# A gated spectral mixer on one core: first half products from 32-bit operands, row tiles normalised one by one, new due times, and a last down product in three parts

## The chip, the cores and the metric

The kernel runs on one core of a Trainium2 chip. The core has five engines with a queue each: PE (matrix products, with its weight loads shown as PEld), DVE (vector work), ACT (activations and copies), POOL, and SP, which here issues all transfers between DRAM and the core's memory. Each engine works through its queue in order; semaphores make one wait for another. The metric is the device time of one execution in microseconds (us), the median of several runs.

## What is computed

The reference has two halves that meet in the last line. `x` is 1 x 2048 x 512.

```python
def _A_ref(x, w_r, w_i):                       # 2-D real FFT over (S, D), filter, inverse
    X = rfft2(x); X = X * (w_r + 1j * w_i); return irfft2(X)

def _B_ref(x, W_gate, W_up, W_down):           # 512 -> 1376 -> 512
    gate = einsum("bsd,df->bsf", x, W_gate)
    up   = einsum("bsd,df->bsf", x, W_up)
    gate = gate * (gate > 0)
    return einsum("bsf,fd->bsd", gate * up, W_down)

xn = _layernorm(x)
return x + _A_ref(xn, A_w_r, A_w_i) * _silu(_B_ref(xn, B_W_gate, B_W_up, B_W_down))
```

## The kernel before

**Tiles.** The 2048 rows are 16 row tiles of 128, loaded two at a time as x0 to x7. The feed-forward half works on four blocks c of four row tiles each (512 columns of PE's output), and on eleven feature tiles f of 128 (the last has 96). `product(c, f, i)` is one such product, i = 0 for the gate weights and 1 for the up weights; its result is the PSUM tile gu{c}_{f}_{i}. `rectify` and `hidden` make the hidden tile h from it, `down(c, f, rows)` multiplies h with the down weights into dn{c}_{row tile}, and `gate` applies the silu.

**Precision.** Everything is multiplied as pairs of 16-bit numbers, a high part and a remainder ("low"): a product of two such pairs takes three passes (`PASSES`: high x high, high x low, low x high). For the first layer one product is 4 blocks of 128 input features x 3 passes = 12 instructions. So before a product can start, x must be normalised, transposed and split (xT, high by ACT and low by DVE), and the weights must be scaled and split: `squares` on ACT sums the squares of the raw weights, `group_scale` adds them over the partitions with a product with `ones` on PE and makes a power of two of it on DVE (p), `group_split` writes the high part (ACT or DVE) and the low part (DVE) into wgu. Weights come in seven groups, raw0 to raw6, of which 0, 1 and 2 hold one feature tile each.

**The start.** x0 (row tiles 0 and 1) is normalised: `stats` makes mean and variance on DVE, `deviation` the inverse deviation with small DVE steps around a root on ACT, for both row tiles in one go, then `normalise` (row tile 0 on DVE, row tile 1 on ACT). `turn_row` transposes them on PE into head0, from which xT is copied. Block 0's feature tiles 0 and 1 (`HALF` = 2) are multiplied in two halves: row tiles 0 and 1 first, 256 columns, then row tiles 2 and 3 when x1 is there. Until PE has work, `keep_busy` fills it with products of `ones` into the PSUM tile small, 79 of them.

**The transform.** The FFT half is a chain of stages per chunk: first_stage (PE tile s1_, results t1_, written to a DRAM tile A_d), then per chunk q loads `at` from A_d and stages y, xx, z, v (results t9_, written to C_d), then last_stage (ct loads, PE tile s2_). The s, v and y stages use 64-wide parts of PE's array.

**What sets the order.** Each piece of work is a `step` with an engine, a cost, the names it reads and writes, and a due time. `Plan.run` plays all steps through a small model of the engines, buffers and transfers: a free engine takes, of the steps that can begin, the one due first. Products get due times from a running clock (`tick`, from `T0`); transform stages from constants (`FIRST`, `MID`, `LAST` with a constant step each); loads from `LOADS` and a lead. The order so found is then what each engine's queue holds. All instructions pass one helper, so the profile gives line 65 for all of them, and groups are told apart by the names of tiles.

**The end.** The last row tile's down product is made in two parts of 256 columns (`columns`, dn3_3 and dn3_3b), so that silu, product with the transform's result sv, sum with x and the store of the first part run while PE makes the second.

The lines that set the widths and the order of that last row tile:

```python
    return (slice(0, 256), slice(256, D)) if (c, i) == (NBL - 1, 3) else (slice(0, D),)
    order = [(f, 2, 0) for f in range(NFT)] + [(f, 3, part) for part in range(2) for f in range(NFT)]
```

Of the kernel before, what the change touches and what calls it, by code (L numbers as in the profile page):

```python
# [32 lines left out]
T0, DOWN, FIRST, FIRST_STEP, MID, MID_STEP, LAST, LAST_STEP = 1.2, 94.9, 53.3, 17.6, 150.3, 18.1, 292.6, 10.8  # L33
LOADS, LOADX = [4.2, 0, 4.4, None, None, None, None], [-2.7, -0.3]
FOLDS, FOLD_LEAD, MARGIN = ['DVE', 'DVE', 'DVE', 'DVE', 'DVE', 'DVE', 'DVE', 'DVE'], 67.8, 1.95
# [3 lines left out]
BUSY, LATE, PAIR1, PAIR2 = 79, 0.4, 0, 0  # L39
SQUARES, HALF = 32.82, 2  # L40
HURRY, SLOW, SLOW_TO = -2, 1, 20
LOWS = [("DVE", "DVE")] * 8

# [4 lines left out]
def columns(c, i):  # L48

    return (slice(0, 256), slice(256, D)) if (c, i) == (NBL - 1, 3) else (slice(0, D),)  # L50
# [184 lines left out]
def kernel(ctx: ExitStack, tc: tile.TileContext, x, wg, wu, wd, wl, ew, sp, c_r, c_d, c_m, c_x, c_s, out):  # L235
# [39 lines left out]
    warm = cpool.tile([P, 1], F32, name="warm")  # L275
    ACT.activation(warm, ones[:, 0:1], AF.Sqrt)
# [25 lines left out]
    def load_x(c):  # L302
        tile_of(f"x{c}", "k4", [P, 2, D], F32)
        if c == 1:
            after_first(("x1", 0), lambda: T["x1"][:, 0, 0:1])
        for i in range(1 + (c == 0)):
            rows = slice(i, i + 1) if c == 0 else slice(0, 2)
            step("SP", .5, lambda rows=rows: SP.dma_start(T[f"x{c}"][:, rows], x[:, 2 * c + rows.start:2 * c + rows.stop, :]),
                 writes=[(f"x{c}", i)], lead=14 if c else None, kb=256 * (rows.stop - rows.start), lag=2.2, due=(LOADX[c] + i * .01) if c < 2 else None)
# [4 lines left out]
    def stats(c, q, j):  # L314
# [6 lines left out]
        tile_of(f"mv{c}", "mv", [P, 2, 2], F32)  # L321
        for i in range(2):
            step("DVE", .82, lambda i=i: run(i), reads=x_names(c, i), writes=[(f"st{c}", i), (f"mv{c}", i)])

    def deviation(c):

        tile_of(f"q{c}", "q", [P, 4, 2], F32)

        def first():
            q = T[f"q{c}"]  # L330
            DVE.tensor_scalar(q[:, 0], T[f"mv{c}"][:, :, 1], EPS, -4.0 / XS ** 2, op0=ALU.add, op1=ALU.mult)

        def last():
            ve, sq, y, t = (T[f"q{c}"][:, i, :] for i in range(4))
            DVE.reciprocal(y, sq)
            for i in range(2):
                DVE.scalar_tensor_tensor(t[:, i:i + 1], y[:, i:i + 1], ve[:, i:i + 1], y[:, i:i + 1],
                                         op0=ALU.mult, op1=ALU.mult)
            DVE.scalar_tensor_tensor(y, t, 3.0, y, op0=ALU.add, op1=ALU.mult)
            if "ACT" in NORM[c]:  # L340
                DVE.scalar_tensor_tensor(ve, T[f"mv{c}"][:, :, 0], -1.0, y, op0=ALU.mult, op1=ALU.mult)
        step("DVE", .13, first, reads=[(f"mv{c}", 0), (f"mv{c}", 1)], writes=[f"q{c}"], port=True)
        step("ACT", .11, lambda: ACT.activation(T[f"q{c}"][:, 1], T[f"q{c}"][:, 0], AF.Sqrt, scale=-1.0),
             reads=[f"q{c}"], writes=[(f"q{c}", 1)])
        step("DVE", .78 + .14 * ("ACT" in NORM[c]), last, reads=[(f"q{c}", 1)], writes=[(f"q{c}", 2)], port=True)
        return f"q{c}", 0
# [19 lines left out]
    def normalise(c, q, at, engines=("DVE", "DVE")):  # L366
# [9 lines left out]
        for i in range(2):  # L376
            e = engines[i]
            step(e, .62 if e == "ACT" else dve2(512), lambda i=i: run(i), reads=[*x_names(c, i), (f"mv{c}", i), (q, 2)],
# [27 lines left out]
    def turn_row(c, i):  # L406
# [13 lines left out]
        step("PE", .45, run, reads=[(f"xf{c}", i)], writes=[(f"head{c}", i)])  # L420
# [66 lines left out]
    def load_group(g):  # L487
        w = sum(fwidth(f) for f in GROUPS[g])
        for i, src in enumerate((wg, wu)):
            tile_of(f"raw{g}_{i}", "k4", [P, 4, w], F32)  # L490
            if g == 1 and not i:
# [3 lines left out]
                 reads=["go"] if g else [], writes=[f"raw{g}_{i}"], lead=12 if g else None, kb=2 * w, lag=2.5, due=LOADS[g])  # L495
# [11 lines left out]
    def group_scale(g):  # L507
        nf = len(GROUPS[g])
        if g > 1:
# [680 lines left out]
```

## Time and profile before

| What | us |
|---|---|
| Runs: median of 3 (lowest, highest) | 409.06 (409.02, 409.29) |
| Profiled execution: span from first to last instruction | 407.1 |
| Median of the runs less that span | 1.96 |
| PE busy in the span | 401.4 (99%) |
| DVE busy | 304.0 (75%) |
| ACT busy | 188.0 (46%) |
| POOL busy | 46.7 (11%) |

The profile is one execution. Its span runs from the first to the last instruction; what lies around it is part of the runs' time and not in the trace. PE's clock was granted in full throughout (1.000). A row of the timeline is "start, length, engine, line, operation, output <- inputs, partitions x elements, how many", and in brackets the idle time of that engine before it and who ended it. A group's length runs from the start of its first instruction to the end of its last, and products overlap at their ends, so the distance between the starts of two groups is the better price. "PEld" is the weight load of a product, "SPq" the time in which SP issues a transfer.

### The profile page before, as it was taken

Reading aid. Unit: us, or ns where it says so; the run is one execution under the profiler, and the core shown is the slowest. Engines: PE = TensorE matmul, PEld = TensorE weight load, DVE = VectorE, ACT = ScalarE, POOL = GpSimd, SP = SyncE. Lnnn points to the kernel's source line nnn. Section 1 sums busy time; section 2 is a strip of 40 time slices with the busy share of each in tenths; the row PEclk is TensorE's granted clock in tenths of the full one; section 3 lists DMA queues with packets and bytes.
Section 4 is the critical chain, followed back from the end, with each engine's and each line's share of the span. In section 5 each row is a group of like instructions: output and inputs, shape, how many; then the busy total and the mean of one; then the engine's idle time right before and its main releaser. Section 6 shows DMA issues by size and latency. Waiting matters only on the chain.

```text
span 407.1 us, 7606 instructions
## 1 busy us (share of the span) xinstructions
PE 401.4 (99%) x2992; PEld 211.5 (52%) x2992; DVE 304.0 (75%) x647; ACT 188.0 (46%) x358; POOL 46.7 (11%) x72
## 2 busy tenths in 40 slices
PE   8999999999999999999999999999999999999995
PEld 7864444444444445455465455546555444444555
DVE  4897986998798979706987578686792328987974
ACT  4999823743467636222355433534523336242411
POOL 0000000000000000001612032030330008040300
PEclk9999999999999999999999999999999999999999
DMA  7980002218549608690006540324201297563242
GB/s 244 403 304 1 0 2 109 54 52 208 171 152 305 172 15 209 128 291 13 2 0 191 173 144 0 100 92 149 52 2 52 61 242 182 161 185 105 103 156 103
DMA packets 36291, 51.78 MB, mean 127 GB/s; under 512 B 15840, under 2 KB 17600, under 8 KB 36256
## 3 DMA queue, kind: packets, MB, share of 16 engines
q1 hardware_dynamic: 36256, 51.31, 42.5%
q8 instruction: 23, 0.38, 0.4%
q14 instruction: 12, 0.10, 0.1%
HBM read 35.55 MB, written 12.60 MB: 118 GB/s over the span
## 4 chain that ended last, share of the span: by engine, by line
PE 97%; ACT 1%; DVE 1%; issue 0%
PE gu L65 55%; PE dn L65 27%; PE s L65 3%; PE z L65 3%; PE xx L65 3%; PE small L65 2%; PE y L65 2%; PE v L65 2%; PE dn_3b L65 1%; ACT xT L65 1%; ACT wgu L65 0%; PE head L65 0%; DVE xT L65 0%; PE sum L65 0%; DVE p L65 0%
## 5 line engine op out<-in xcount | busy, mean ns | idle before, releaser
L65 PE MATMUL gu<-xT,wgu 128*128 128x512 f16 (+1 forms) x1008 | 213.3, 369 | 0.4 <-DVE xT L65 0.4
L65 PEld LDWEIGHTS <-wgu 128*128 128x128 f16 x1008 | 97.5, 98 | 107.5 <-issue 3.5
L65 PE MATMUL dn<-wds,h 128*128 128x512 f16 (+2 forms) x528 | 115.8, 373 | 0.0
L65 PEld LDWEIGHTS <-h 128*128 128x128 f16 (+1 forms) x561 | 53.7, 98 | 57.3 <-issue 2.0
L65 DVE TENSOR_TENSOR h<-gu,r 128x512 f32<-128x512 f32 (+2 forms) x52 | 33.6, 646 | 24.2 <-PE gu L65 22.9
L65 ACT ACTIVATE h<-h 128x512 f16<-128x512 f32 (+1 forms) x44 | 27.5, 626 | 51.0 <-DVE h L65 51.0
L65 POOL TENSOR_TENSOR po<-tt,tt 128x256 f32<-128x256 f32 x16 | 14.4, 900 | 262.6 <-DVE tt L65 208.7
L65 ACT ACTIVATE r<-gu 128x512 f32<-128x512 f32 (+1 forms) x44 | 26.2, 595 | 36.5 <-PE gu L65 36.3
L65 DVE TENSOR_TENSOR h<-h,h 128x512 f16<-128x512 f32 (+1 forms) x44 | 29.7, 689 | 5.3 <-ACT h L65 5.1
L65 DVE SCALAR_TENSOR_TENSOR tt<-xsp,cw,wt 128x512 f32<-128x512 f32 x32 | 25.3, 847 | 0.0
L65 POOL TENSOR_TENSOR ae<-zz 128x128 f32<-128x128 f32 (+1 forms) x32 | 17.8, 593 | 62.8 <-ACT zz L65 47.9
L65 ACT ACTIVATE g<-dn,cdi 128x512 f32<-128x512 f32 (+1 forms) x16 | 10.6, 673 | 23.9 <-PE dn L65 23.9
L65 PE MATMUL gu<-xT,wgt 128*64 128x256 f16 (+1 forms) x144 | 17.0, 309 | 0.0
L65 DVE TENSOR_TENSOR sv<-sv,g 128x512 f32<-128x512 f32 (+1 forms) x17 | 11.2, 690 | 6.4 <-ACT g L65 6.1
L65 DVE TENSOR_TENSOR t<-v,t 128x1024 f16<-128x1024 f32 x8 | 9.8, 1219 | 7.9 <-ACT t L65 7.9
L65 DVE TENSOR_TENSOR z<-z,z 128x1024 f16<-128x1024 f32 x8 | 9.7, 1218 | 7.5 <-ACT z L65 7.5
L65 ACT ACTIVATE z<-z 128x1024 f16<-128x1024 f32 x8 | 8.2, 1024 | 15.2 <-PE z L65 15.2
L65 POOL TENSOR_TENSOR pf<-tt,tt 128x256 f32<-128x256 f32 x16 | 14.0, 888 | 7.7 <-PE gu L65 7.7
L65 ACT ACTIVATE p<-pf 128x1024 f16<-128x1024 f32 x8 | 8.4, 1056 | 13.0 <-DVE pf L65 13.0
L65 DVE SCALAR_TENSOR_TENSOR wgu<-raw,p,wgu 128x512 f16<-128x512 f32 x20 | 14.4, 745 | 0.1
L65 ACT ACTIVATE xs<-xs 128x1024 f16<-128x1024 f32 x8 | 8.3, 1052 | 12.8 <-DVE xs L65 9.3
L65 ACT ACTIVATE wgu<-raw 128x512 f16<-128x512 f32 x20 | 12.3, 619 | 3.7 <-DMA raw<-in_wg 3.7
(134 smaller groups left out, 430.6 us busy)
## 6 DMA issues: line engine op xcount, KB each, us to landing
A_d<-t SPq DMA_DIRECT2D x16, 256.0 KB, 3.3
rw<-in_wl SPq DMA_DIRECT2D x8, 512.0 KB, 5.1
wt<-in_wl SPq DMA_DIRECT2D x8, 512.0 KB, 4.8
at<-A_d SPq DMA_DIRECT2D x8, 512.0 KB, 4.9
C_d<-t SPq DMA_DIRECT2D x16, 256.0 KB, 3.3
ct<-C_d SPq DMA_DIRECT2D x16, 256.0 KB, 5.6
xt<-in_x SPq DMA_DIRECT2D x16, 256.0 KB, 4.3
out<-xt SPq DMA_DIRECT2D x15, 256.0 KB, 2.1
```

What stands on the lines that cost most here:

```text
L65: return lambda *args, **kw: self.tc.keep_in_program_order(f(*args, **kw))
```

## The change

Four things change.

1. **32-bit half products.** For block 0 and feature tiles 0 and 1, the half for row tiles 0 and 1 is no longer made from split 16-bit numbers. `turn_row` copies the transposed x as 32-bit numbers (xTf0 by ACT, xTf1 by DVE), and `product` multiplies the raw 32-bit weights with it: four 128-column products for each row tile, each weight matrix and each of the two feature tiles, 32 in all. Their scale differs from that of the other half, so `rectify` and `hidden` work on these tiles in two halves with different factors (p and the new `ups`). xT is then split from xTf. Feature tile 1's results move from the tag dn to F.
2. **Row tiles one by one.** For x0, `deviation` runs once for each row tile (`ALONE`), and the statistics of row tile 1 are made by ACT (`STATS`: a sum, its negative mean, a sum of squared differences), not by DVE.
3. **Due times.** The transform stages get a due time each in place of a constant step, loads a lead each, and most constants of the model change. `keep_busy` makes 42 filler products in place of 79.
4. **The end.** The last row tile's down product has three parts of 256, 128 and 128 columns (dn3_3, dn3_3b, dn3_3bb).

```diff
-T0, DOWN, FIRST, FIRST_STEP, MID, MID_STEP, LAST, LAST_STEP = 1.2, 94.9, 53.3, 17.6, 150.3, 18.1, 292.6, 10.8
+FIRSTS = [58.53, 65.2, 93.07, 106.1, 121.7, 135.1, 152.7, 170.3]
...
-BUSY, LATE, PAIR1, PAIR2 = 79, 0.4, 0, 0
+BUSY, LATE = 42, 0.4
...
+ALONE, EVAC, WHOLE = (((0,), (1,)), ((0, 1),)), ("ACT", "DVE"), .95
+HALVES, HEADS, STATS = ('gu', 'F'), [None, 8.91], ((0, 1),)
...
-    return (slice(0, 256), slice(256, D)) if (c, i) == (NBL - 1, 3) else (slice(0, D),)
+    return (slice(0, 256), slice(256, 384), slice(384, D)) if (c, i) == (NBL - 1, 3) else (slice(0, D),)
...
         for i in range(2):
+            if (c, i) in STATS:
+                st, mv, of, junk = (lambda: T[f"st{c}"]), (lambda: T[f"mv{c}"]), (lambda: T[f"x{c}"][:, i, :]), (lambda: T[f"xf{c}"][:, i, 0:D])
+
+                step("ACT", .75, lambda: ACT.activation(junk(), of(), AF.Copy, accum_out=st()[:, 6:7]),
+                     reads=x_names(c, i), writes=[(f"st{c}", 2), (f"xf{c}", i)])
+                step("ACT", .2, lambda: ACT.activation(st()[:, 7:8], st()[:, 6:7], AF.Copy, scale=-1.0 / D),
+                     reads=[(f"st{c}", 2)], writes=[(f"st{c}", 3)])
+                step("ACT", .8, lambda: ACT.activation(junk(), of(), AF.Square, bias=st()[:, 7:8], accum_out=st()[:, 8:9]),
+                     reads=[*x_names(c, i), (f"st{c}", 3)], writes=[(f"st{c}", i), (f"xf{c}", i)])
+                step("DVE", .13, lambda: DVE.tensor_scalar(mv()[:, i, :], st()[:, 6:9:2], 1.0 / D, None, op0=ALU.mult),
+                     reads=[(f"st{c}", i), (f"st{c}", 2)], writes=[(f"mv{c}", i)])
+                continue
...
+        if c == 0:
+            n = f"xTf{i}"
+            tile_of(n, "k2", [P, 4, P], F32)
+            e, act_ = EVAC[i], lambda: ACT.activation(T[n].rearrange("p k r -> p (k r)"), head(), AF.Copy)
+            step(e, (dve if e == "DVE" else act)(512), act_ if e == "ACT" else lambda: DVE.tensor_copy(T[n].rearrange("p k r -> p (k r)"), head()),
+                 reads=[(f"head{c}", i)], writes=[n])
+            of = lambda: T[n].rearrange("p k r -> p (k r)")
+            step("ACT", act(512), lambda: ACT.activation(xt(0), of(), AF.Copy), reads=[n], writes=[(f"xT{c // 2}", j, 0)])
+            step("DVE", dve(512), lambda: DVE.tensor_sub(xt(1), of(), xt(0)), reads=[n, (f"xT{c // 2}", j, 0)],
+                 writes=[(f"xT{c // 2}", j, 1)], port=True)
+            return
...
+        if c == 0 and f < HALF and rows.start == 0:
+            def whole(j):
+                for k in range(4):
+                    matmul(to()[:, j], T[f"raw{g}_{i}"][:, k, :], T[f"xTf{j}"][:, k, :], start=k == 0, stop=k == 3)
+            for j in range(2):
+                step("PE", WHOLE, lambda j=j: whole(j), reads=[f"xTf{j}", f"raw{g}_{i}"], writes=[(name, 0, i)], due=tick(WHOLE))
+            sums[c, f, i] = to, [(name, k, i) for k in range(2)]
+            return
...
+        elif c == 0 and f < HALF:
+            step("DVE", stt(256), lambda: DVE.scalar_tensor_tensor(h32()[:, 0:2], up()[:, 0:2], ups[:, f:f + 1], r()[:, 0:2], op0=ALU.mult, op1=ALU.mult),
+                 reads=[U[0], (f"r{c}_{f}", 0), f"p{f}"], writes=[n32], due=clock[0] + 3)
+            step("DVE", dve(256), lambda: DVE.tensor_mul(h32()[:, 2:4], up()[:, 2:4], r()[:, 2:4]), reads=[U[1], (f"r{c}_{f}", 1)], writes=[n32], due=clock[0] + 3)
...
-            first_stage(k, FIRST + FIRST_STEP * (k | PAIR1))
+            first_stage(k, FIRSTS[k])
...
-                product(0, f, i, slice(2 * h, 2 * h + 2), ("gu", "dn", "F")[f])
+                product(0, f, i, slice(2 * h, 2 * h + 2), HALVES[f])
```

**What stands where: PE at the start.** Before, on PE, from the first column sum to the first useful product. 45 of the filler products ("small<-ones") stand ahead of head0, which is both row tiles, and 24 more behind it:

```order
L65 MATMUL small_119<-m0_168,ones_94 128x2
...
L65 MATMUL head0_214<-unit_76,xf0_201 128x128 x8
L65 LDWEIGHTS ones_94
L65 MATMUL small_119<-ones_94 128x256
...
L65 LDWEIGHTS wgu0_77
L65 MATMUL gu0_0_0_274<-xT0_233,wgu0_77 128x256
```

Now, on PE, from the first transpose (37 fillers ahead, five behind it) to the second half of feature tile 0 (gu0_1 is feature tile 1, both weight matrices in one tile):

```order
L73 MATMUL gu0_0_0_218<-xTf0_209,raw0_0_129 128x128 x4
L73 MATMUL gu0_0_1_231<-xTf0_209,raw0_1_134 128x128 x4
L73 MATMUL head0_197<-unit_76,xf0_157 128x128 x4
L73 MATMUL gu0_1_245<-xTf0_209,raw1_0_153 128x128 x4
L73 MATMUL small_120<-m0_189,ones_94 128x2
L73 MATMUL gu0_0_0_218<-xTf1_251,raw0_0_129 128x128 x4
L73 MATMUL gu0_0_1_231<-xTf1_251,raw0_1_134 128x128 x4
L73 MATMUL gu0_1_245<-xTf1_251,raw1_0_153 128x128 x4
L73 MATMUL head1_293<-unit_76,xf1_274 128x128 x8
L73 MATMUL gu0_1_245<-xTf0_209,raw1_1_166 128x128 x4
L73 MATMUL gu0_1_245<-xTf1_251,raw1_1_166 128x128 x4
L73 MATMUL small_120<-m1_236,ones_94 128x2
```

The row tiles are transposed apart, raw weights stand as operands, and no filler product stands behind the first 32-bit one.

**DVE behind it.** Before, on DVE, from the low part of the first weight matrix to that of the third:

```order
L65 SCALAR_TENSOR_TENSOR wgu0_77<-raw0_0_128,p0_210,wgu0_77 128x512
L65 TENSOR_TENSOR xT0_233<-head0_214,xT0_233 128x512 x2
L65 TENSOR_SCALAR q1_271<-mv1_221 128x2
L65 TENSOR_SCALAR p1_287<-small_119 128x2
L65 TENSOR_SCALAR p1_287<-p1_287 128x2 x2
L65 SCALAR_TENSOR_TENSOR wgu0_77<-raw0_1_133,p0_210,wgu0_77 128x512
L65 TENSOR_SCALAR wgu1_78<-raw1_0_152,p1_287 128x512
```

Now, on DVE, from the normalisation of x1 to the high parts of feature tile 1:

```order
L73 TENSOR_SCALAR xf1_274<-x1_149,mv1_225,q1_239 128x512
L73 TENSOR_TENSOR xT0_267<-xTf0_209,xT0_267 128x512
L73 SCALAR_TENSOR_TENSOR wgu0_77<-raw0_0_129,p0_269,wgu0_77 128x512
L73 SCALAR_TENSOR_TENSOR wgu0_77<-raw0_1_134,p0_269,wgu0_77 128x512
L73 TENSOR_TENSOR xT0_267<-xTf1_251,xT0_267 128x512
L73 TENSOR_TENSOR xT0_267<-head1_293,xT0_267 128x512 x2
L73 SCALAR_TENSOR_TENSOR h32_0_0_324<-gu0_0_1_231,ups_101,r0_0_299 128x256
L73 TENSOR_SCALAR p1_341<-small_120 128x2
L73 TENSOR_SCALAR p1_341<-p1_341 128x2 x2
L73 TENSOR_SCALAR ups_101<-p1_341 128x1
L73 TENSOR_SCALAR wgu1_78<-raw1_0_153,p1_341 128x512
L73 TENSOR_SCALAR wgu1_78<-raw1_1_166,p1_341 128x512
```

x1 is normalised ahead of all low parts, and the four x remainders stand on both sides of the first weights'.

**SP around A_d.** Before, on SP, the last writes of A_d, the transposes of x6 and x7, and the first loads from A_d:

```order
L65 DMA A_d<-t_6_1957 128x1x1024 x2
L65 DMA A_d<-t_7_1966 128x1x1024 x2
L65 DMA_TRANSPOSE xT_2012<-x_6_1693 128x16x128
L65 DMA_TRANSPOSE xT_2012<-x_7_1744 128x16x128
L65 DMA at_2071<-A_d 128x2x1024
```

Now, on SP, the same place:

```order
L73 DMA row_mw<-mw 128x1
L73 DMA cm_1884<-in_c_m 128x512
L73 DMA wt_1914<-in_wl 128x1024
L73 DMA_TRANSPOSE xT_1825<-x_7_1761 128x16x128
L73 DMA A_d<-t_6_1912 128x1x1024 x2
L73 DMA A_d<-t_7_1923 128x1x1024 x2
L73 DMA rows_mw<-row_mw 128x128
L73 DMA cm_1977<-in_c_m 128x512
L73 DMA wt_1914<-E_d 2x2x128
L73 DMA wt_2005<-in_wl 128x1024
L73 DMA at_2017<-A_d 128x2x1024
```

Both transposes have moved ahead of the writes, and three small loads and a scale's row stand between the writes and the first load.

90 lines of the change are left out of this document (56 added, 34 removed).

## The prediction

> **What bounds the kernel now.** I read the page's busy shares first, then who waited for whom on PE, then the timelines of the first 32 us, of the transform stages and of the end. Times are us from the start of the span, "start, length".
>
> ```profile
> span 407.1 us, 7606 instructions
> PE 401.4 (99%) x2992; PEld 211.5 (52%) x2992; DVE 304.0 (75%) x647; ACT 188.0 (46%) x358; POOL 46.7 (11%) x72
> PE gu L65 <- DVE xT L65: 0.4, 1, 0.4
> ```
>
> PE is busy 99%, and after its first instruction it waits 0.4 us in all. So a shorter wait elsewhere buys nothing. Time can come only from PE's own queue: filler products that become useful ones, cheaper stage changes, a shorter end. The first matters most, because "small<-ones" is filler:
>
> ```profile
> 1.05 6.42 PE L65 MATMUL small<-ones 128*128 128x256 f16 x38 [1.05 <-DVE md L65]
> 8.46 1.04 PE L65 MATMUL head<-unit,xf 128*128 128x128 f32 x8
> 9.33 2.78 PE L65 MATMUL small<-ones 128*128 128x256 f16 x24
> 12.69 2.78 PE L65 MATMUL gu<-xT,wgu 128*128 128x256 f16 x24
> 15.99 1.47 PE L65 MATMUL gu<-xT,wgu 128*128 128x256 f16 x12
> 18.86 1.58 PE L65 MATMUL gu<-xT,wgu 128*128 128x256 f16 x13
> 20.83 18.24 PE L65 MATMUL gu<-xT,wgu 128*128 128x256 f16 x107 [0.39 <-DVE xT L65]
> ```
>
> From 20.83 on the useful work never stops. Feature tiles 0 and 1 are 96 products of 256 columns; 24 + 12 + 13 = 49 are done by then and 47 are left. One takes 0.108 (2.78 / 24 is 0.116, but the group's length ends with the drain of its last product, some 0.17). So the first product of feature tile 2 (gu0_2_0) starts at 20.83 + 47 x 0.108 = 25.9. That is the mark: whatever moves it moves the end, as long as nothing later waits.
>
> **The start.** The change computes the first half (two row tiles of four) of tiles 0 and 1 from 32-bit operands: eight groups of four 128-column products, where 48 products of 256 columns stood (48 x 0.108 = 5.2). They need no scale, no split weights and no split x. No 32-bit product of this size is in the trace; the nearest rows are the transposes (above, 8.46) and the column sums:
>
> ```profile
> 8.35 0.90 PEld L65 LDWEIGHTS head<-unit,xf 128*128 128x128 f32 x8
> 12.22 0.30 PEld L65 LDWEIGHTS small<-m,ones 128*128 128x128 f32 x2 [0.39 <-ACT wgu L65]
> 12.36 0.21 PEld L65 LDWEIGHTS <-ones 128*128 128x128 f16 x2
> ```
>
> A 32-bit transpose of 128 columns, with a new weight load each (x8), goes every (9.33 - 8.46) / 8 = 0.11. A 32-bit column sum is one instruction in the program and two here (x2), both in 12.36 - 12.22 = 0.14. So a 32-bit product should be two passes. Lower end: 0.14, if only the two loads counted. Upper end: 2 x 0.22 = 0.44, if a pass took twice a transpose. I take 2 x 0.11 = 0.22, since the transpose has the same columns and the same load: 0.88 for a group, 7.0 for eight, 1.8 more than now. [...]
>
> Now when the groups can start, from these durations:
>
> ```profile
> 3.49 0.69 DVE L65 BATCH_NORM_STATS2 st<-x 128x6 f32<-128x512 f32 x1 [2.47 <-DMA x<-in_x]
> 5.97 0.63 ACT L65 ACTIVATE wgu<-raw 128x512 f16<-128x512 f32 x1 [3.75 <-DMA raw<-in_wg]
> 7.68 0.54 DVE L65 TENSOR_SCALAR xf<-x,mv,q 128x512 f32<-128x512 f32 x1
> 8.86 0.37 DVE L65 TENSOR_SCALAR p<-p 128x2 int32<-128x2 int32 x2
> 9.89 1.07 ACT L65 ACTIVATE xT<-head 128x512 f16<-128x512 f32 x2
> 11.43 1.28 DVE L65 TENSOR_TENSOR xT<-head,xT 128x512 f16<-128x512 f32 x2
> 22.77 0.48 DVE L65 TENSOR_SCALAR wgu<-raw,p 128x512 f16<-128x512 f32 x1
> 24.70 2.07 DVE L65 SCALAR_TENSOR_TENSOR wgu<-raw,p,wgu 128x512 f16<-128x512 f32 x3
> ```
>
> Row tile 0 is now normalised alone. Its statistics start at 3.49 as before; with them, five small DVE steps of 0.18 (8.86, two in 0.37), a root on ACT and the 0.54 it is ready near 6.1, not at 7.68 + 0.54 = 8.2. But 37 filler products stand ahead on PE, until about 7.1 (38 ended at 7.5, the last 16 or so at 0.108, drain 0.17); they, not the data, hold the transpose. Transposed by 7.65 and copied by ACT (0.6) it is there at 8.3, the weights since 5.97 and after. Then PE in the order shown: two groups 10.1, second transpose 10.5, a group and a sum 11.5, three groups 14.2, eight transposes of x1 15.1, two groups and a sum 17.0. ACT, one step of 0.63 of squares and one normalisation after 8.3, has the second row tile ready at 9.7, so PE runs through.
>
> The second half needs split x and split weights, and there DVE is late. From the second transpose (drained 10.65): copy 0.64, five small steps of x1's deviation 0.9, scale in four steps 0.7, normalise 0.54 = 13.4; an x remainder 0.64 = 14.1. ACT meanwhile has nine steps of 0.63 after 8.3 before the first high weights are there, at 14.2. Two weight remainders at 0.69 = 15.6, three x remainders at 0.64 = 17.6. So PE waits 0.65, then 24 products to 20.25. Tile 1's weights: a half product 0.4, scale 0.7, two high parts 0.48, two remainders 0.69 = 21.1, each before PE comes to it, so 24 products to 23.0, a sum, and gu0_2_0 at 23.3. Six handovers between engines that I left out, at 0.03 (below, from 403.06 + 0.47 to 403.56), make it 23.5: **2.4 us earlier** than 25.9. ACT's three new statistics steps, an extra root, a copy and the halved rectifiers are about 3 us more on ACT, which is full early and free after 50:
>
> ```profile
> 20.00:30.00 10.00, 9.61 (x71) 6.70 (x69) 9.86 (x26) 9.64 (x26) 0.00 (x0) 1.00 0.93 321
> 50.00:60.00 10.00, 10.00 (x48) 4.57 (x47) 9.45 (x19) 2.42 (x4) 0.00 (x0) 1.00 0.02 2
> ```
>
> (Columns: stretch, length, then PE, PEld, DVE, ACT, POOL.) The cover of those 3 us is this slack. What is late next, with an earlier PE and a fuller ACT, are the scaled weights of tile 7: by the same bookkeeping DVE has them within 0.4 of when PE asks. I cost that at 0.1, inside the rounding, and keep it for the range.
>
> **The transform stages.** New due times move the stages. A stage that uses part of the array costs extra on entry and exit. First two groups of 24 full products from the chain, the first ahead of a v stage, the second between full products; then the s stages:
>
> ```profile
> 213.07 5.29 PE gu L65 x24
> 311.43 5.18 PE gu L65 x24
> 67.99 1.51 PE L65 MATMUL s<-xs,cR 64*64 64x257 f16 x48
> 69.44 4.20 PE L65 MATMUL gu<-xT,wgt 128*128 128x512 f16 x36
> 100.86 0.85 PE L65 MATMUL s<-xs,cR 64*64 64x257 f16 x24
> 101.65 1.47 PE L65 MATMUL dn<-wds,h 96*128 96x512 f16 x6
> ```
>
> To enter costs 5.29 - 5.18 = 0.11. A single s stage takes 0.79, two in a row 1.45: merging saves 2 x 0.79 - 1.45 + 0.11 = 0.24. By the order, excursions into such stages fall from 26 to 21: s1_2 with s1_3, s1_4 with s1_5, v0 with v1, y4 with y5 (4 x 0.24, with v and y taken like s), and unlike neighbours gain three places and lose two (0.11 each): about 1.0; I take **0.95 us**, if nothing new waits. The place to look is the first y stage, which reads A_d:
>
> ```profile
> 158.81 1.60 PE L65 MATMUL s<-xs,cR 64*64 64x257 f16 x48
> 165.49 2.99 SPq L65 DMA_DIRECT2D A_d<-t  x4
> 168.53 6.72 SPq L65 DMA_TRANSPOSE xT<-x  x2
> 175.45 1.54 SPq L65 DMA_DIRECT2D at<-A_d  x3
> 179.75 0.20 DVE L65 COPY am<-at 128x126 f16<-128x126 f16 x1 [6.83 <-DMA at<-A_d]
> 180.77 0.23 PE L65 MATMUL y<-cm,at 64*128 64x64 f16 x4
> ```
>
> Now y starts 20.4 after the last s (158.81 + 1.6), 1.0 after its data. By the order 78 full products at 0.216 and the narrow last tile (1.5) stand between: 18.3. But both transposes now go ahead of the last A_d writes on SP. With the present 5.1 from s to the first write (a transpose of 3.36 fits into it), 3.0 of issue, 4.3 for the landing as for the load, and 4.3 for the load it is 16.7, so 1.6 are spare though y comes earlier. The other due times and leads I cost at nothing: DVE is busy 75%, and PE comes to each stage with several 2.59 products between.
>
> **The end.** The last row tile's product is 256 + 128 + 128 columns instead of 256 + 256.
>
> ```profile
> 279.95 1.51 PE L65 MATMUL z<-cD,p 128*128 128x128 f16 x24
> 281.30 2.10 PE L65 MATMUL dn<-wds,h 128*128 128x512 f16 x9
> 396.83 0.69 ACT L65 ACTIVATE g<-dn,cdi 128x512 f32<-128x512 f32 x1 [7.13 <-PE dn L65]
> 403.06 0.47 ACT L65 ACTIVATE g<-dn_3b,cdi 128x256 f32<-128x256 f32 x1 [2.15 <-PE dn_3b L65]
> 403.56 0.42 DVE L65 TENSOR_TENSOR sv<-sv,g 128x256 f32<-128x256 f32 x1 [1.74 <-ACT g L65]
> ```
>
> A 128-column product takes (281.30 - 279.95) / 24 = 0.056, so 66 for 33 cost 66 x 0.056 - 33 x 0.108 = +0.13. ACT goes from 0.69 to 0.47 for half the columns, so to 0.36 for a quarter; DVE from 0.64 (11.43, two in 1.28) to 0.42, so to 0.31, in the product and again in the sum behind it. That saves 3 x 0.11 = 0.33, and half the last transfer perhaps 0.1. Net **-0.30**. The middle part ends 18 products (1.0 us) ahead, so its steps have left ACT and DVE in time.
>
> **The sum.** -2.4 - 0.95 - 0.30 = -3.65 against the span of 407.1, which is 1.96 under the runs' median of 409.06; the part outside the span is taken as unchanged: 409.06 - 3.65 = 405.4. Of the bounds, 0.14 per 32-bit product gives little, since DVE then sets the start (0.6 more), and a better end or fuller merging 0.5: 404.3.
>
> **Rivals.**
> 1. *The 32-bit product costs double (0.44).* 32 x 0.22 = 7.0 more, less the 0.65 wait it fills: +6.35, 411.8, slower than before. It decides at (3.65 + 0.65) / 32 = 0.13 more each, so from 0.35 on. For it: a transpose need not do all that a product does. Against: two passes are already counted. [...] Chance 0.11.
> 2. *DVE is later than my sum in the second half*, since its steps wait for ACT one by one (each x remainder waits for a copy of ACT): half of the start's gain goes, 406.6. For it: DVE 9.86 of 10 and ACT 9.64 of 10 busy from 20 to 30. Chance 0.20.
> 3. *A stage waits in the middle*: a result one product late costs 2.59 and leaves 408.0. Against it: no such wait now with like spacing, and 1.6 spare at y. Chance 0.10.
> 4. *The earlier mark is eaten again* by the weights of tiles 5 to 8 behind ACT's extra 3 us: 408.3 to 409, no change. Against it: 2.42 of 10 from 50 on. Chance 0.05.
>
> The forecast itself has 0.54. A measurement of this kernel tells 0.2% (0.8 us) from no change. Faster: 0.54 + 0.20 and most of rival 3 = 0.82; same, rival 4 and a little of 3: 0.06; slower, rival 1 and a double wait: 0.12. The range 404.3 to 408.3 leaves out rivals 1 and 4 and the far end of 3.
>
> **What would show it.** Right: gu0_2_0 near 23.5; 32-bit groups every 0.88 from 8.3; one PE wait of about 0.6 near 17 for x remainders; no PE wait after 30; single s and v stages in pairs; the last product about 3.3 earlier. Wrong: groups of 1.7, waits on DVE longer than 1.5 before 24, or any PE wait beside y, z or v.

## The result, and the profile after

The changed kernel is **slower**: 419.24 us (median of 5 runs, 418.02 to 419.43) against 409.06 (408.8 to 409.41), a ratio of 1.0244 with a 95% interval of 1.0231 to 1.0256. The forecast was 405.4. The profiled execution took 418.02 with a span of 416.2, 9.1 more than the 407.1 of before.

First the page of the changed kernel (head, busy shares, and from its second part PE and the granted clock), then the table of who waited for whom on PE:

```profile
span 416.2 us, 7641 instructions
PE 401.3 (96%) x3004; PEld 213.0 (51%) x3004; DVE 305.0 (73%) x656; ACT 190.4 (46%) x368; POOL 47.8 (11%) x72
PE   8999999899999998949999999999999999999996
PEclk9999999999999999988999999999999999999999
```

```profile
PE y L73 <- DMA at<-A_d: 5.8, 1, 5.8
PE gu L73 <- DVE h L73: 2.2, 2, 1.6
PE dn L73 <- DVE wds L73: 1.5, 3, 0.8
```

PE is as busy as before (401.3 against 401.4), so no work was added on balance; it waits instead. The hole is the 4 in PE's row of slices, and the clock's row has two eights there. PE's timeline of the changed kernel shows the four places (start, length; the wait ahead in brackets):

```profile
23.46 1.47 PE L73 MATMUL gu<-xT,wgu 128*128 128x256 f16 x12 [0.57 <-DVE h L73]
24.91 13.11 PE L73 MATMUL gu<-xT,wgu 128*128 128x512 f16 x60
...
72.31 4.28 PE L73 MATMUL dn<-wds,h 128*128 128x512 f16 x19
77.38 1.46 PE L73 MATMUL dn<-wds,h 128*128 128x512 f16 x6 [0.79 <-DVE wds L73]
...
159.20 2.75 PE L73 MATMUL gu<-xT,wgu 128*128 128x512 f16 x12 [1.63 <-DVE h L73]
...
172.63 9.24 PE L73 MATMUL dn<-wds,h 128*128 128x512 f16 x42
187.63 0.29 PE L73 MATMUL y<-cm,at 64*128 64x64 f16 x4 [5.75 <-DMA at<-A_d]
...
191.03 2.76 PE L73 MATMUL dn<-wds,h 128*128 128x512 f16 x12
```

In the kernel before, the same two first y stages end here:

```profile
182.76 4.71 PE L65 MATMUL dn<-wds,h 128*128 128x512 f16 x21
```

The 9.1 us add up as follows:

- **Waits behind the mark, +8.9**: dn on DVE wds 1.5 (three), gu on DVE h 1.6, the first y 5.75. Before, PE waited for nothing after 20.83.
- **Drains, +0.8**: 19 products of 0.216 are 4.10, but from 72.31 to the start of the wait (77.38 - 0.79 = 76.59) it is 4.28. Each of these five waits costs such a drain beside itself, about 0.16 (at 0.216 each, the rows of 6 products in 1.46 and of 12 in 2.75 leave 0.16).
- **Down products behind the third wait, +0.9**: the 101 products from 81.01 to 103.80 take 22.79; at the pace of before (132 in 28.61) they would take 21.9. The table of waits shows nothing there, but from 82 to 90 PE is busy 7.65 us with 35 products, before 8.00 with 39. From 80.2 to 86.4 DVE starts the last step of one feature tile's down weights every 1.54, and the six products of one such tile take 1.30: by this reading PE goes at the pace of the weights.
- **The first y stages, +1.4**: two of them take 191.03 - 187.63 = 3.40; the same two take 182.76 - 180.77 = 1.99 before. Experiment 5 shows why.
- **Gains, -2.9**: gu0_2_0 starts at 24.91 and not 25.9 (-1.0); the end, from the start of the last down products to the end of the span, takes 25.78 and not 26.37 (-0.6; experiment 1 has 0.4); what is left of the sum, -1.3, falls to the transform stages. The s, v and y stages alone, from start to start and with the low clock taken out, take 0.7 less; the rest was not read apart.

8.9 + 0.8 + 0.9 + 1.4 - 2.9 = 9.1.

**Behind the first y** stands this row of events on SP (SPq: the time in which SP issues), with one line of the view of DMA issues from 159 to 176 (KB each, us to landing):

```profile
163.31 0.35 SPq L73 DMA_DIRECT2D row_mw<-mw  x1
...
164.23 1.40 SPq L73 DMA_DIRECT2D wt<-in_wl  x1
165.72 9.28 SPq L73 DMA_TRANSPOSE xT<-x  x1
175.10 3.20 SPq L73 DMA_DIRECT2D A_d<-t  x4
...
181.69 1.54 SPq L73 DMA_DIRECT2D at<-A_d  x3
```

```profile
row_mw<-mw SPq DMA_DIRECT2D x1, 0.5 KB, 8.0
```

The data of the last writes was complete at 168.09 on DVE (the low parts of t1_6 and t1_7 run from 166.60 for 1.49). The writes left at 175.10, since SP sat 9.28 us in one transpose; before, two transposes at this place took 6.72 together, 3.36 each. Beside that transpose, for 8.0 us, ran row_mw: 128 single numbers, 0.5 KB. Before, it had been issued at 141.09, far from any transpose. The wait is explained by the transpose's place in SP's queue, by its length, or by both; experiments 3 and 4 part these.

**The 1.63 near 159** has another source. In the chain of work that ended last, one row is

```profile
147.34 8.13 DMA xT<-x
```

This is an earlier transpose, issued right behind loads of the filter (rw); DVE's steps for xs wait for it until 155.49, and the h for which PE waits stands behind them. When the filter's due time goes back (experiment 3), this wait goes too; when row_mw alone moves (experiment 4), it stays at 2.07.

### The profile page after: what moved, and what is told of

Read it like the earlier page. It is cut to its first block, busy times and chain, and to the rows that moved or that the text cites. A ratio compares the mean times of both kernels' runs of the same rounds, so it can differ in the third digit from the quotient of the medians.

```text
span 416.2 us, 7641 instructions
## 1 busy us (share of the span) xinstructions
PE 401.3 (96%) x3004; PEld 213.0 (51%) x3004; DVE 305.0 (73%) x656; ACT 190.4 (46%) x368; POOL 47.8 (11%) x72
## 4 chain that ended last, share of the span: by engine, by line
PE 75%; DVE 12%; DMA 8%; ACT 2%; SPq 2%; issue 1%; DVEq 0%
PE gu L73 40%; PE dn L73 21%; PE z L73 3%; PE xx L73 3%; DVE h L73 2%; PE s L73 2%; DMA row_md<-md 2%; DVE wgu L73 2%; PE y L73 2%; DMA xT<-x 2%; DVE wds L73 2%; PE small L73 2%; DVE xs L73 2%; SPq L73 2%; PE v L73 2%; DMA at<-A_d 1%
## 5 line engine op out<-in xcount | busy, mean ns | idle before, releaser
L73 PE MATMUL gu<-xT,wgu 128*128 128x512 f16 (+1 forms) x960 | 208.3, 374 | 2.7 <-DVE h L73 2.2
L73 PEld LDWEIGHTS <-wgu 128*128 128x128 f16 x960 | 92.9, 98 | 109.6 <-issue 5.9
L73 DVE TENSOR_TENSOR h<-gu,r 128x512 f32<-128x512 f32 (+3 forms) x52 | 33.1, 636 | 29.5 <-PE gu L73 28.0
L73 ACT ACTIVATE r<-gu 128x512 f32<-128x512 f32 (+2 forms) x44 | 25.7, 584 | 47.2 <-PE gu L73 47.1
L73 POOL TENSOR_TENSOR ae<-zz 128x128 f32<-128x128 f32 (+1 forms) x32 | 20.1, 661 | 62.8 <-ACT zz L73 62.7
L73 ACT ACTIVATE a<-y 128x1024 f16<-128x1024 f32 x8 | 8.1, 1022 | 17.6 <-PE y L73 17.5
L73 DVE TENSOR_TENSOR a<-y,a 128x1024 f16<-128x1024 f32 x8 | 9.8, 1221 | 7.4 <-ACT a L73 7.4
L73 DVE TENSOR_TENSOR sv<-sv,g 128x512 f32<-128x512 f32 (+2 forms) x18 | 11.3, 661 | 4.8 <-ACT g L73 4.6
L73 ACT ACTIVATE t<-v 128x1024 f16<-128x1024 f32 x8 | 8.1, 1022 | 13.1 <-PE v L73 13.1
L73 PE MATMUL y<-cm,at 64*128 64x64 f16 x384 | 8.3, 201 | 5.8 <-DMA at<-A_d 5.8
```

The lines of the kernel that those rows point to most:

```text
L73: return lambda *args, **kw: self.tc.keep_in_program_order(f(*args, **kw))
```

## Experiment 1: the end alone

The kernel before with the last product in three parts.

```diff
-    return (slice(0, 256), slice(256, D)) if (c, i) == (NBL - 1, 3) else (slice(0, D),)
+    return (slice(0, 256), slice(256, 384), slice(384, D)) if (c, i) == (NBL - 1, 3) else (slice(0, D),)
...
-for part in range(2) for f in range(NFT)]
+for part in range(len(columns(c, 3))) for f in range(NFT)]
```

> The kernel before with the last row tile's product in three parts, and nothing else of the change. By the prediction's sum -0.30 us, so 408.8 by the median of 409.06. Rival: the last step is a transfer whose length does not fall with its size, so that only the 66 short products count, +0.1, 409.2. If the end has a share in the 10.2 us by which the changed kernel is slower, this kernel is over 410.

Measured: 408.46 against 408.87 for the kernel before on the same chip, ratio 0.9987 (0.9977 to 0.9997). The end brings about 0.4 (by the interval between 0.1 and 0.9), as priced; it has no share in the loss.

## Experiment 2: the due times alone, the start alone

First the kernel before with the new due times, then the changed kernel with those of before:

```diff
 before, with the new due times:
+T0, DOWN, FILTER, TICK = 2.22, 96.244, 153.189, 1.169
+FIRSTS = [58.53, 65.2, 93.07, ...]
...
 changed, with those of before:
-T0, DOWN, FILTER, TICK = -0.157, 96.244, 153.189, 1.169
+T0, DOWN, FILTER, TICK = -1.17, 94.9, 138.3, 1.17
+FIRSTS = [53.3 + 17.6 * k for k in range(8)]
...
```

> The kernel before with the new due times of the stages, of the filter's scale, of the down weights and the new fold lead, but its own start and end; the clock of the first product is set so that every product from feature tile 2 on has the due time of the changed kernel. Theory: the new due times make the loss, since they put PE, SP and DVE in an order in which PE waits beside down products, gate products and the first y; then this kernel is slow without any 32-bit product: 413 to 419, with waits of PE on DMA at<-A_d or DVE h of several us. Rival: the 32-bit start makes ACT and DVE late, and these delays run on to the y stage; then this kernel gains the merged stages and has about 408.

> The changed kernel with the due times of the stages, of the filter's scale, of the down weights and the fold lead of before, and the end in two parts; the start with 32-bit products stays. Theory (the due times make the loss): the start keeps the 1.0 us that gu0_2_0 is earlier in the changed kernel, and nothing waits more than 0.5 later on: 408.1, between 407.6 and 409. Rival (ACT's extra steps make the down weights late): PE waits on DVE wds for 1 to 2 us near 75, 409 to 410.5. If the start alone makes the loss: above 415.

Measured: the due times alone 413.07 (ratio 1.0100, 1.0084 to 1.0117), the start alone 412.41 (1.0080, 1.0063 to 1.0098). Who waited for whom on PE, due times alone, then start alone:

```profile
PE y L70 <- DMA at<-A_d: 3.5, 1, 3.5
```

```profile
PE dn L73 <- ACT wds L73: 1.9, 1, 1.9
PE dn L73 <- DVE wds L73: 1.3, 2, 0.8
PE gu L73 <- DVE wgu L73: 1.2, 1, 1.2
```

Each half of the change is slower by itself, by 4.2 and by 3.5 us, and at different places: the due times at the first y, the start at the down weights. Of the start my first theory fell (408.1 expected). Its rival names the right place, but with 3.2 us of waits at the down weights and not 1 to 2, so the time lies above its range (409 to 410.5) as well. With the due times alone, row_mw leaves at 155.46 and lands after 10.13; SP then holds the load of its copies (rows_mw) until 165.61, and the last two transposes and the last writes to A_d stand behind that. By its chain of work the same row thus delays the first y in another way. So two causes have to be found, not one.

## Experiment 3: one due time, and SP's order alone

The changed kernel with the filter's due time of before, then the changed kernel with the last transpose behind the loads from A_d:

```diff
-T0, DOWN, FILTER, TICK = -0.157, 96.244, 153.189, 1.169
+T0, DOWN, FILTER, TICK = -0.157, 96.244, 138.3, 1.169
```

```diff
-        step("SP", 3.4, run, reads=[(f"x16_{c}", i, h) for i in range(2) for h in range(2)], 
+        step("SP", 3.4, run, reads=[...] + [("A_d", c, i) for i in range(2) if c == NCH - 1],
...
-        step("SP", .6, lambda: SP.dma_start(rows, row.broadcast_to([P, P])), reads=[f"row_{name}"], ...
+        step("SP", .6, lambda: SP.dma_start(rows, row.broadcast_to([P, P])), reads=[f"row_{name}"], lead=-6.2 if name == "mw" else None, ...
```

> The changed kernel with one number changed: the due time of the filter's scale is 138.3, as before, and not 153.19. By the order the eight filter loads then stand on SP ahead of the last three transposes, and the last four writes to A_d stand ahead of the last two transposes. Theory: the late filter loads share the DMA with the transposes, SP stays in the last one for 9.28 us, and the A_d writes behind it are late; then the wait of 5.75 ahead of the first y goes, with it the low clock behind it (1.9), and most of the 1.63 on DVE h near 159: 419.2 - 5.75 - 1.9 - 1.0 = 410.5, between 409.5 and 412. Rival: y is simply due too early, whatever SP does: the wait stays over 3 us, 415 or more.

> The changed kernel with the order of SP alone altered at one place: the last transpose goes behind the three loads from A_d, and the row of the filter's maximum behind the last four writes to A_d; the filter loads and all due times stay. Theory (order): the writes to A_d are held by the 9.28 us of the transpose in front of them, nothing else; they leave at about 168.5 and not 175.1, the loads land near 181.5, and the first y waits 0 to 0.5, not 5.75; without the idle time no low clock: 419.2 - 5.5 - 1.9 = 411.8, between 411 and 413. Rival (the DMA itself is full there): the writes land late all the same, the wait stays over 3 us, 416 or more.

Measured: 410.74 (ratio 1.0042, 1.0028 to 1.0057) with the earlier filter, 1.9 above the kernel before on the same chip, so one number takes away 8.3 of the 10.2 us; the first y waits 0.2 and DVE h near 159 no more, while two waits beside s (1.1) are new. But the order alone gives 418.02, still 9.2 above the kernel before: the rival's outcome came, the writes land late all the same. SP of that kernel, its first y on PE, and a piece of its chain of work (start, length):

```profile
163.80 0.35 SPq L73 DMA_DIRECT2D row_mw<-mw  x1
...
168.45 3.37 SPq L73 DMA_DIRECT2D A_d<-t  x4
```

```profile
185.78 0.29 PE L73 MATMUL y<-cm,at 64*128 64x64 f16 x4 [4.71 <-DMA at<-A_d]
```

```profile
170.48 8.74 DMA A_d<-t
```

The writes now leave at 168.45, at once behind their data, and yet one of them takes 8.74 to land, so that the loads wait for it until 179.2. In the kernel before a write to A_d landed after 4.0 in the median of this place. A load of 512 KB issued 0.9 behind row_mw (wt) took 11.4. So the place of the transpose is not what decides: a transpose, a write and a load were each slow behind row_mw.

## Experiment 4: the 128 single numbers moved

The transpose stays ahead of the writes; row_mw goes behind the loads from A_d.

```diff
-        step("SP", .6, lambda: SP.dma_start(row.rearrange("a p -> p a"), col), reads=reads, writes=[f"row_{name}"], due=due, kb=8, lag=3.)
+        step("SP", .6, lambda: SP.dma_start(row.rearrange("a p -> p a"), col), reads=reads, writes=[f"row_{name}"], due=due, lead=-15.9 if name == "mw" else None, kb=8, lag=3.)
```

> The changed kernel with row_mw<-mw (128 single numbers, 8.0 us to landing) issued behind the loads from A_d and not 2.4 us ahead of the last transpose; the transpose stays ahead of the A_d writes. Theory (collision): the transpose lasts 9.28 since it shares the DMA with these single numbers; without them it lasts 2 to 3.4 us as elsewhere, the writes leave near 169, and the wait of the first y falls below 1 us: 411 to 413. Rival: the transpose is long for another cause (the filter load in front of it), stays above 6 us, and y waits 4 us or more: 416 to 419.

Measured: 412.48 (ratio 1.0091, 1.0071 to 1.0111). SP of this kernel:

```profile
164.60 2.87 SPq L73 DMA_TRANSPOSE xT<-x  x1
167.56 3.24 SPq L73 DMA_DIRECT2D A_d<-t  x4
...
173.86 1.41 SPq L73 DMA_DIRECT2D at<-A_d  x3
175.31 0.48 SPq L73 DMA_DIRECT2D row_mw<-mw  x1
```

```profile
169.74 4.11 DMA A_d<-t
```

(The last line is from its chain of work.) The transpose lasts 2.87, with the same filter load (wt) in front of it; the write lands after 4.11; the first y does not wait. The cause of the 5.75 us is thus shown from both sides: a transfer of 0.5 KB in 128 pieces, in flight beside the transpose and the writes. (That it is the pieces, and not something else about this transfer, was not tested.) A new wait appears (xx on DVE a, 2.2), because on DVE the filter's scale, which now has its row only at 190.9, stands ahead of that step; 3.7 us remain above the kernel before, where the changed kernel had 10.2.

## Experiment 5: the clock behind the hole

Filler products of 256 columns in the hole; they compute nothing that is used.

```diff
         def y_stage():
             y = T[f"y{q}"]
+            if q == 0:
+                for _ in range(54):
+                    matmul(y[:, 0].rearrange("p t b c -> p (t b c)")[:, 0:256], ones.bitcast(F16)[:, 0:P], ones.bitcast(F16), start=True, stop=True)
```

> The changed kernel with 54 filler products of 256 columns (54 x 0.108 = 5.8 us) ahead of the first y stage, which computes nothing that is used. They end about when the data lands, so the data is not earlier. Theory (clock): the 3.47 us of the first two y stages, against 1.51 for two others, come from the low granted clock that follows the idle time; with fillers the clock stays 1.0, the two stages take 1.5, and the kernel has 419.2 - 1.9 = 417.3, or 417.8 if the fillers end 0.5 late. Rival: they are slow because the second block of data lands late: 3.4 us again, 419 to 420.

Measured: 417.05 (ratio 1.0203, 1.0182 to 1.0223; two executions), 8.2 above the kernel before on the same chip and not 10.2, though its data lands no earlier. By windows (stretch, length, PE busy, granted clock, DMA share, GB/s), first the changed kernel, then the one with fillers:

```profile
182.00:184.00 2.00, 0.00 (x0) 1.00 0.84 238
184.00:186.00 2.00, 0.00 (x0) 0.53 0.96 298
...
188.00:190.00 2.00, 2.00 (x70) 0.50 0.47 178
190.00:192.00 2.00, 2.00 (x44) 0.76 0.00 0
```

```profile
188.00:190.00 2.00, 1.63 (x89) 1.00 0.50 194
```

PE's timeline with fillers, from the first y stage on:

```profile
187.75 0.23 PE L73 MATMUL y<-cm,at 64*128 64x64 f16 x4 [0.26 <-DMA at<-A_d]
189.47 0.87 PE L73 MATMUL y<-cm,at 64*128 64x64 f16 x48 [0.37 <-DMA at<-A_d]
190.28 2.76 PE L73 MATMUL dn<-wds,h 128*128 128x512 f16 x12
```

In the changed kernel PE went idle at 181.88; from about 184.1 the granted clock is 0.5, and it stays there until about 191, 3.3 us into the work that follows. With fillers it stays 1.0, and the two stages take 190.28 - 187.75 = 2.53 and not 3.40; 0.37 of this is a wait for the second block of data, so the rival has a small share too. The expected 1.5 was taken from two later y stages; these first two take 1.99 in the kernel before as well. In the two profiled executions the fillers bring 0.74, almost all of it here. That the medians differ by more was not followed up.

## Experiment 6: the late sum behind the down weights

The down weights are scaled by one factor, which needs the maxima of all weights (md), which need the scale of the last weight group, which needs its column sum on PE. Before, the last sums stand at 41.64 and the row of the maxima leaves at 50.22; in the changed kernel:

```profile
41.64 0.50 PE L65 MATMUL sum<-m,ones 128*128 128x4 f32 x4
50.22 0.33 SPq L65 DMA_DIRECT2D row_md<-md  x1
59.47 0.32 SPq L65 DMA_DIRECT2D rows_md<-row_md  x1
65.34 0.23 DVE L65 TENSOR_SCALAR scd<-rho,pd 128x11 f32<-128x11 f32 x1
```

```profile
51.08 0.28 PE L73 MATMUL sum<-m,ones 128*128 128x4 f32 x2
54.25 0.33 SPq L73 DMA_DIRECT2D row_md<-md  x1
63.35 0.33 SPq L73 DMA_DIRECT2D rows_md<-row_md  x1
69.40 0.23 DVE L73 TENSOR_SCALAR scd<-rho,pd 128x11 f32<-128x11 f32 x1
```

(The first fence is the kernel before.) The sum is 9.4 later, the factor 4.1 (before, DVE took up the last of these sums only at 46.45), while PE comes to dn 1.3 earlier (72.31 and not 73.56). Both edits start from the kernel with the earlier filter: first an early due time for the sums and, by the planner's rule, all that they need; then for the PE step of the sums alone.

```diff
-             reads=[(f"m{g}", j, i) for j in range(nf) for i in range(2)], writes=[name])
+             reads=[(f"m{g}", j, i) for j in range(nf) for i in range(2)], writes=[name], due=24 if g > 4 else None)
```

```diff
+        for s in steps:
+            s.due = min(s.due, s.early)
...
+        s.early = 20 if g > 4 else 1e9
```

> The kernel with the filter's due time of before (410.74) and one more edit: the column sums of the last two weight groups get an early due time, so that by the order the last one stands behind 224 units of feature work on PE (a unit is 0.108 us) and not behind 320; in the kernel before it is 240. Theory: the scale of the down weights hangs on that sum; with it some 8 us earlier the row of the maxima leaves near 46 and not 54, the down weights are in time, the three waits of dn on DVE wds (1.6) go: 410.7 - 1.6 = 409.1, and 408.5 if fewer waits beside s follow. Rival: ACT's extra steps of the start make the squares late, so PE then waits for the sum's data, or DVE is late with the gate weights: 410 to 411.

> The changed kernel with the filter's due time of before (410.74 measured) and the early due time for the PE step alone of the last two column sums, so that the loads and squares ahead of them keep their order, which they did not in the kernel of 409.56. Theory: the three waits of dn on DVE wds (1.6) and their drains (0.5) go and the start stays at 24.1 to 24.9: 408.6, between 408.0 and 409.4; what then still stands above the kernel with the due times of before are the waits beside s and the first y that the new due times leave. Rival: the waits only move from the down weights to the gate weights: 410 or more.

Measured: 409.56 (ratio 1.0019, 1.0001 to 1.0037) and 408.36 (1.0008, 0.9975 to 1.0041; the ten executions lie between 406.78 and 412.2). In both the waits on DVE wds are gone; in the second the last sum stands at 45.23, and PE is busy for all of the 8 us from 82 to 90. In the kernel with the start alone (experiment 2) the last sum stands at 57.05, later than in the changed kernel, and its waits at the down weights are longer (3.2 and not 1.5). The first lost part of it again at the start (1.1 on DVE xT and 0.8 on ACT xT), since squares and loads moved too. PE's waits behind the start in the second:

```profile
PE s L73 <- DVE xs L73: 0.5, 2, 0.3
PE y L73 <- DMA at<-A_d: 0.2, 1, 0.2
```

The sum's place on PE is therefore the cause of the dn waits. ACT's extra steps alone are not: with the same steps and an earlier sum, nothing waits there.

## Experiment 7: all old due times, and the loads ahead of both transposes

First the changed kernel with the due times of before, moved by 1.0 with its clock, and the early sums; last the kernel of 408.36 with both transposes behind the loads from A_d:

```diff
-T0, DOWN, FILTER, TICK = -0.157, 96.244, 153.189, 1.169
+T0, DOWN, FILTER, TICK = -0.157, 95.9, 139.3, 1.17
+FIRSTS = [54.3 + 17.6 * k for k in range(8)]
+MIDS = [151.3 + 18.1 * k for k in range(8)]
...
+        s.early = 20 if g > 4 else 1e9
```

```diff
-        step("SP", 3.4, run, reads=[(f"x16_{c}", i, h) for i in range(2) for h in range(2)], 
+        step("SP", 3.4, run, reads=[...] + [("A_d", NCH - 1, i) for i in range(2) if c >= NCH - 2],
```

> The changed kernel (32-bit start, end in three parts) with the due times of the stages, of the filter's scale, of the down weights and the fold lead of before, all 1.0 later as the clock of its products is, and with an early due time for the PE step alone of the last two column sums: by the order the last one stands behind 272 units of feature work (a unit is 0.108 us), 320 in the changed kernel, 240 before. Theory: three things made the loss, each removed here: the down weights' scale hung on that late sum (1.52 and its drains), the single numbers of the filter's maximum ran beside the transposes (5.75 and the low clock behind it), and DVE waited for a transpose near 155 (1.63). What is left is the start (gu0_2_0 1.0 to 1.8 earlier than before) and the end (-0.4 measured alone): 409.0 - 1.4 - 0.4 = 407.2, between 406.6 and 408.0. Rival: the start's extra steps on ACT and DVE cost as much later as they bring: 408.3 to 409.5, with waits on DVE or ACT between 40 and 90.

> The kernel with the early sums and the filter's due time of before (408.36, its executions at 406.8 to 408.7 with a clock of 0.998 to 1.0 and at 410.8 to 412.2 with 0.995 to 0.996), with SP's order altered as well: both last transposes go behind the three loads from A_d, which they held until 176.31, though the writes had landed near 173. Theory: in the slower executions the first y, which came 0.24 late in the profiled one, waits so long that the low clock follows; with the loads about 3 us earlier no execution does, and all lie between 406.3 and 408.0, median 407.2, below the kernel before by about 1.6. Rival: the long wait is elsewhere (at the s stage near 158, behind a transpose), and executions of 410 to 412 remain, median 408 to 409.

Measured: 414.51 (ratio 1.0140, 1.0118 to 1.0163), so this theory fell: the old due times do not bring back the old order. PE and ACT of that kernel near 155, and the clock:

```profile
156.82 4.12 PE L73 MATMUL gu<-xT,wgu 128*128 128x512 f16 x12 [2.29 <-ACT r L73]
155.23 1.06 ACT L73 ACTIVATE xs<-xs 128x1024 f16<-128x1024 f32 x1 [10.43 <-DMA xT<-x]
158.00:160.00 2.00, 2.00 (x7) 0.51 0.00 0
```

(The second line is ACT's, the third a window.) On SP its transpose left at 149.28, behind the row of the filter's maximum, which had to wait for row_mw until 148.86; ACT stood 10.43 us for that transpose, the rectifier behind it was late, PE idled 2.29 us, and 12 products then took 4.12 and not 2.75, most of this time at half the clock.

The last kernel has 407.86 against 408.76, ratio 0.9985 (0.9968 to 1.0003). The loads leave at 172.18 and the first y does not wait, as expected; the executions lie closer (406.53 to 410.35), but five of twelve are above the 408.0 that was expected as the upper end, and two of them above 410, one at full clock. So the wait of the first y is not the whole reason for the slower executions. The ratio is the lowest of all these kernels, but its interval holds 1; of the kernels tried, only the one with the three-part end alone has an interval below 1 (0.9977 to 0.9997), and only just.

## Why the prediction was wrong

**The start: mechanism right, size off by 1.4.** Two 32-bit groups take 10.99 - 9.11 = 1.88, so 0.94 each and 0.235 for a product, where 0.22 was taken and rival 1 had 0.44 (all eight take 7.3 in sum, where 7.0 was taken):

```profile
9.11 2.05 PE L73 MATMUL gu<-xTf,raw 128*128 128x128 f32 x16
10.99 0.60 PE L73 MATMUL head<-unit,xf 128*128 128x128 f32 x4
9.10 1.86 PEld L73 LDWEIGHTS gu<-xTf,raw 128*128 128x128 f32 x16 [0.42 <-ACT xTf L73]
```

A pass is 0.117 with its weight load inside (16 loads in 1.86), where each of the eight transposes, with a load too, took 0.11. gu0_2_0 came at 24.91 and not 23.5: the fillers ended later (the first group at 9.11 and not 8.3), and DVE h, which my bookkeeping had in time, held PE for 0.57. The later end of the fillers is most likely chance: PE starts them at half its later pace (10 in the first 2 us) and goes over to 0.108 each at a moment that differs from profile to profile. From 5 to 7 us it starts 13 products in the changed kernel, 19 in the kernel before, 19 in the kernel of experiment 5, whose start is that of the changed kernel, and 21 in the two kernels of 408.36 and 407.86. Those two have the same start; their 37 fillers take 5.9 and 6.0 us and not 6.93, and gu0_2_0 comes at 24.24 and 23.98, 1.7 and 1.9 earlier than before.

**Rival 4 came, at another place.** "The earlier mark is eaten again" had the gate weights of tiles 5 to 8 in mind and 0.05 of chance. It was the down weights, and not through ACT's extra 3 us but through the place of a column sum of two passes on PE. The prediction had not followed the chain from sums to down weights at all, so it put nothing for this; it cost about 2.9 (waits 1.5, their drains 0.5, the slower pace behind them 0.9).

**The transform stages: the gain came, the spare did not exist.** The rarer excursions gave about 1.3 by what is left of the sum, where 0.95 was taken. The step that failed is "the present 5.1 from s to the first write (a transpose of 3.36 fits into it)": the transpose took 9.28, the time from s to the first write became 11.8 (163.32 to 175.10), and "1.6 are spare" became a wait of 5.75, with a price of 1.4 in clock and about 0.16 in drain. The order of SP that stands ahead of the prediction has row_mw three rows ahead of that transpose; the prediction gives this row no cost, though in the kernel before it took 7.3 from issue to landing. With it fell "The other due times and leads I cost at nothing": one of them, the filter's, is worth 8.3 us; with it went the wait of 1.63 near 159 too.

**Rival 3 had the right place and the wrong size.** It named a stage that waits in the middle, with y as the place to look, but priced it as one product late (2.59) and gave it 0.10. The wait that came was for a transfer, and 5.75 long.

**The end** was right: -0.30 expected, -0.4 measured. One sign that the prediction named for a wrong forecast was seen, a PE wait beside y, and one that it named for a right one failed, no PE wait after 30.

## What to carry to other kernels

Price a moved transfer by its time to landing and by what is issued behind it, not by its size: here 0.5 KB in single numbers took 8.0 us to land, where a load of 512 KB from A_d took 6.6 in the median, and the transpose behind it took 9.28 and not the 2.87 that it took at that place without it. When a change makes PE wait where it was never idle, add the drain (about 0.16 here) and the low clock that may follow (here behind waits of 2.29 us and more, not behind those of 2.17 and less). And before a start is made faster, follow the longest chain that the later work hangs on back to its first step: where that step stands in the engine's order decides, not how busy the engines are.

## What the runs showed of the hardware

- **What was issued behind row_mw was slow.** row_mw (0.5 KB) took 7.3 us to landing before, 8.0 in the changed kernel and 11.2 in experiment 4. Behind it a transpose took 9.28 on SP (9.52 in experiment 5), and 2.87 at the same place without it; elsewhere in these kernels a transpose that stands alone in SP's rows took 1.65 to 6.36; a write to A_d landed after 8.74 behind it and after 4.11 without. The other such row, of the down weights, took 9.0 in the changed kernel and 9.2 with the start alone.
- **Low clock behind a wait, from 2.29 us on.** PE waits of 2.29 (experiment 7, first kernel), 3.50 (experiment 2, due times alone), 4.71 (experiment 3, order alone) and 5.75 us (changed kernel) were followed by a granted clock of 0.5, beginning 2.3 to 3.7 us after PE went idle and lasting up to 5.0 us into the next work; waits of 1.63 (changed kernel), 1.86 (experiment 2, start alone), 2.07 and 2.17 (experiment 4) left it at 1.0.
- **How long the low clock lasted.** By the clock records of the traces, the low stretches behind these four waits last 3.41, 3.41, 6.83 and 6.83 us, and the stretches of full clock ahead of them 177.49 (three times) and 153.60: all whole multiples of 3.413. What follows is my estimate from these lengths. If each trace is cut into steps of that length, PE was idle for 2.20, 2.26, 2.92 and 3.26 us of the step just ahead of the low clock. The waits of 1.63 and 1.86 lay in one step each, and those of 2.07 and 2.17 were split between two steps, with at most 1.40 in one. So a bound between 1.86 and 2.20 of idle time within one step fits these eight waits; a bound between 2.17 and 2.29 of idle time as a whole fits them too (one more step of low clock, behind the wait of 4.71, followed on 1.79 at half clock).
- **Open:** why executions of the kernels of 408.36 and 407.86 differ by up to 5 us, since only one of each was profiled. (Five of the six above 410 have a mean clock of 0.994 to 0.996. By an estimate from the lengths above, one stretch of 3.41 at half clock in a span of 409 gives 1 - 0.5 x 3.41 / 409 = 0.996, so one such stretch of low clock in each is likely; the wait behind it was not seen.) Open is also what a start without the late sum would be worth with the order of before, since no due times brought that order back.
